# Attention, softplus FFN and routed experts on one core: wider mask and weight-conversion operations, setup on another engine, and a new table of due dates

## The chip, the cores and the metric

The program runs on one core of a Trainium2 chip. A core has TensorE (PE, matrix products), VectorE (DVE), ScalarE (ACT), GpSimd (POOL) and SyncE (SP, here the issuer of most transfers), each with an instruction stream of its own that it works through in order. The metric is the device time of the whole program in microseconds (us); lower is better.

## The reference, cut to what matters

```python
# attention: r, k, v are (4, 8, 768, 48), w and u (8, 48)
for t in range(S):
    cur = np.einsum('bhd,bhe->bhde', u[None] * kt, vt)
    y[:, :, t] = np.einsum('bhd,bhde->bhe', rt, state + cur)
    state = w[None, :, :, None] * state + np.einsum('bhd,bhe->bhde', kt, vt)
x = y, heads side by side: (3072, 384)
# FFN, w_in (384, 2048), w_out (2048, 384), both float64
h = x @ w_in
x = (np.maximum(h, 0.0) + np.log1p(np.exp(-np.abs(h)))) @ w_out
# experts: 8 of them, each takes at most 384 tokens, highest logits first
logits = x @ w_gate
(token, expert) pairs in falling order of logit; a token goes to the first expert with room
out[mask_e] = np.maximum(x[mask_e] @ w1[e], 0.0) @ w2[e]      # (384, 1024), (1024, 384)
```

## The kernel before

**Attention** is done in chunks of 64 time steps: 24 steps n, each for two sequences b and 8 heads (4 pairs `pr` of two, q = 0, 1). In a step PE transposes the scaled k and r (`ks`, `rs`) into `kT` and `ar`, `prods` makes 32 products of 64x64 (L516), DVE multiplies them by a triangular mask (`masked`, L524), and further products with `X` (L594) and the state follow. Three steps fill one block of 384 tokens.

**The FFN** takes 8 blocks of 384 tokens; for each of 16 slices f of the hidden size it makes 9 matmuls of 128x384 (L728; three in block 0, in fp32), softplus on ACT (L734 to L736) and DVE (L741, result `gf`), and a split of `gf` into two halves of 16 bits (L348 or L350, and `rest`, L748). The second product (L835 for block 0, L838 to L840) adds over the slices. `w_in` and `w_out` come as pairs of 32-bit words of a float64. `from_double` fetches one slice of 384 columns into one of four buffers `RAW` and makes float32 of it with three DVE operations on bits (L640, L642, L644): 32 slices, 96 operations. `halve_win` and `halve_wout` split the result into two fp16 halves.

**The experts** follow: `select(p)` finds the tokens of expert p by a search over thresholds (PE L1086, L1103, DVE L1073 to L1110), GpSimd gathers their rows (L1255), SP turns them by a transposing transfer (L1330), `up` makes 8 x 9 matmuls (L1342), `relu` (ACT L1346) and `rest` (DVE L1349) split the result, `down` makes 3 x 24 matmuls (L1360 to L1362), GpSimd scatters (L1370). The weights of an expert come in 8 pieces y (four of `w1`, four of `w2`) of 384 KB: `fetch` (SP, L1280) into one of four buffers `mraw` (`RB = 4`), which is free again when the piece four earlier has been converted; `hi` makes the upper half on ACT (L1289), `lo` the lower one on DVE (L1296). For the last two experts seven of the eight pieces are converted in another way (`ON_POOL`): ACT L1286 and L1287, then GpSimd L1294.

**What sets the order.** Nothing runs at once: each step is recorded as an item with an engine (or two that could take it, with a price each), a planned duration, what it depends on, and a due date. `lay_out` (L148) then simulates the engines with these durations and writes each engine's stream in the order that comes out; of the items that could start, the one with the earliest due date goes. Where two engines could take an item, `BIAS` and `YIELD` weigh one against the other. Transfers have a size, by which a single modelled DMA clock advances; an item without a size has a fixed delay `lat`:

```python
            if it.size:
                dma = max(start + 1275.0, dma) + it.size
                it.lat = dma + 1000.0 - it.done
```

`keep_warm` (L135) then puts filler matmuls (L143: zeros, into a bank that nobody reads) wherever the plan has PE idle. On the chip nothing of the plan is left but the order: an engine goes on when what it waits for is there. The plan's numbers stand in tables: `T0`, `LEN0`, `LEN`, `LAST` are the planned times of the FFN blocks, `RAWL`, `BITL`, `WOUTL`, `HALFL`, `HALFL2` how long before its use a weight is fetched, converted and split; `STEP` is the time per expert, `FETCHL`, `HIL`, `LOL`, `W1L`, `W2L` how long before its use a piece of expert weight is fetched and converted, `XLEAD` and `GLEAD` the leads of transposes and gathers.

At the start DVE makes the identities and the mask from an iota of GpSimd (`idents`, L418 to L421), then the table of powers of the decay w (`powers`, L427 to L436), of which PE transposes copies (L453, L459).

Of the kernel before, what the change touches and what calls it, by code (L numbers as in the profile page):

```python
# [21 lines left out]
def tile_kernel(ctx, tc, r, k, v, w, u, w_in, w_out, w_gate, w1, w2, out):  # L22
# [7 lines left out]
    C = 64  # L30
# [220 lines left out]
    T0 = 16250.0  # L251
    LEN0 = 43500.0
    LEN = 25600.0
    NLATE = 12
    EARLY = 0.62
    LATE = [divmod(NB * SPB - NLATE + i, SPB) for i in range(NLATE)]
    LAST = 26100.0
# [71 lines left out]
    RAW = [piece(flat, 4 * i, 4, I32).rearrange("p (m t) -> p m t", t=2) for i in range(4)]  # L329
    WT = [piece(flat, 22 + 2 * i, 2, FT) for i in range(3)]  # L330
# [66 lines left out]
    pw = AR[1].rearrange("p a b c d -> p (a b c d)")[:, :2 * HP * C].rearrange("p (i a c) -> p i a c", i=2, a=HP)  # L397
# [19 lines left out]
    def idents():  # L417
        DVE.tensor_scalar(identf, jp, 0.0, None, op0=OP.is_equal)  # L418
        DVE.tensor_copy(identh, identf)
        DVE.tensor_scalar(mask[0:64], jp[0:64, 0:64], 0.0, None, op0=OP.is_gt)  # L420
        DVE.tensor_scalar(mask[64:128], jp[64:128, 64:128], 0.0, None, op0=OP.is_gt)  # L421

    op("dve", 600.0, idents, r=["jp"], w=["ident"], due=-1e9)


    def powers():
        DVE.tensor_copy(sq[:, 0], wt)  # L427
        for i in range(6):
            DVE.tensor_mul(sq[:, i + 1], sq[:, i], sq[:, i])
        DVE.reciprocal(pw[:, 0, :, 0], sq[:, 5])  # L430
        DVE.tensor_copy(pw[:, 1, :, C - 1], pw[:, 0, :, 0])
        for i in range(6):
            m = 1 << i
            f = sq[:, i, :, None].to_broadcast([128, HP, m])
            DVE.tensor_mul(pw[:, 0, :, m:2 * m], pw[:, 0, :, 0:m], f)
            DVE.tensor_mul(pw[:, 1, :, C - 2 * m:C - m], pw[:, 1, :, C - m:C], f)  # L436
# [12 lines left out]
    op("dve", 3200.0, powers, r=["wt"], w=["pw", ("ar", 1, 0)], due=-1e8)  # L449

    def power_table(i):
        bank = Bank("att")
        op("dve", 335.0, lambda: DVE.tensor_copy(PW2[0], pw[:, i, :, None, :].to_broadcast([128, HP, 2, C])),  # L453
           r=["pw", ("ar", 1, 0)], w=["pw2", ("kT", 1)], due=-1e7)
# [14 lines left out]
    def attention(n):  # L469
# [41 lines left out]
        def prods():  # L511
            pa = [b.view(HP, 64) for b in b3]
# [13 lines left out]

        op("pe", 625.0, prods, r=[("kT", i), ("ar", i, 0), ("ar", i, 1)], w=[("am", i, 0), ("am", i, 1)], due=due + 3, bank=b3, small=True)
        for q in range(2):
            op("dve", 890.0, lambda q=q: masked(q), r=["ident"], w=[("am", i, q)], due=due + 3, bank=b3[q])
# [104 lines left out]
    def from_double(src, t, key, due):  # L634
        c = WN[0]
        WN[0] += 1
        raw = RAW[c % 4]
        op("sp", 450.0, lambda: src(raw), w=[("raw", c % 4)], due=due - RAWL, size=1900.0)
        hi, lo = [raw[..., i] if len(t.shape) == 2 else raw[..., i].rearrange("p (k f) -> p k f", k=KC) for i in (1, 0)]
        op("dve", 269.0, lambda: DVE.tensor_scalar(t, hi, 0x07FFFFFF, 3, op0=OP.bitwise_and, op1=OP.logical_shift_left),  # L640
           r=[("raw", c % 4)], w=[key], due=due - BITL)
        op("dve", 469.0, lambda: DVE.scalar_tensor_tensor(t, hi, -0x40000000, t, op0=OP.bitwise_and, op1=OP.bitwise_or),  # L642
           r=[("raw", c % 4)], w=[key], due=due - BITL)
        op("dve", 469.0, lambda: DVE.scalar_tensor_tensor(t, lo, 29, t, op0=OP.logical_shift_right, op1=OP.bitwise_or),  # L644
           r=[("raw", c % 4)], w=[key], due=due - BITL)

    def prep_win(j):
        from_double(lambda raw: SP.dma_start(
            raw.rearrange("p (k f) t -> p k (f t)", k=KC),
            w_in.rearrange("(k p) f -> p k f", p=128)[:, :, 256 * j:256 * (j + 1)]),  # L650
            WF32[j].bitcast(I32), ("wi", j + 1), due_ffn1(0, j))
# [10 lines left out]
    def prep_wout(f):  # L662
        due = due_ffn2(0, 0, f) - WOUTL
        t = WU32[f]
        from_double(lambda raw: SP.dma_start(
            raw.rearrange("p m t -> p (m t)"), w_out.rearrange("(c p) m -> c p m", p=128)[f]),
            t[:, :DM].bitcast(I32), ("wo", f + 1), due)
# [205 lines left out]
    for f in range(FC):  # L873
        prep_win(f)
# [114 lines left out]
    STEP = 25200.0  # L989
    SPAN = 22300.0  # L990

    ON_POOL = [()] * 6 + [(0, 1, 2, 3, 4, 5, 7)] * 2
    XLEAD = 10900.0
    GLEAD = 17400.0
    FETCHL = 20500.0
    W1L = -5700.0
    W2L = 9500.0
    HIL = 6100.0
    LOL = -11500.0
    DOWNL = 13200.0  # L1000
    INVL = -9500.0
# [247 lines left out]
    def gather(p, need):  # L1249
# [7 lines left out]
        for j in range(3):  # L1257
            old = xts[3 * p + j - 6] if p >= 2 else None
            GI[p].append(item("pool", 1050, lambda j=j: one(j), [SEL[p][3], old, more_room] + need, begin(p) - GLEAD, 2250))
            GI[p][-1].remote = True  # L1260

    def weights(p):
# [37 lines left out]
        for y in range(2 * WQ):  # L1300
# [3 lines left out]
            f = item("sp", 450, lambda y=y: fetch(y), [ld, old], want - FETCHL, size=1092)  # L1304
# [17 lines left out]
    def experts(p):  # L1322
# [90 lines left out]
        for j in range(3):  # L1413
# [11 lines left out]
            ots.append(item("pool", 1100, lambda j=j: scatter(j), [t], begin(p) + DOWNL + 3900 * (j + 1), 2300))  # L1425
# [43 lines left out]
```

## Time and profile before

| | |
|---|---|
| median of three runs | 768.3 us (767.6, 768.3, 773.15) |
| the profiled execution, as timed | 769.4 us |
| its span in the trace | 767.6 us |
| PE busy | 748.2 us, 97% |
| DVE busy | 593.8 us, 77% |
| ACT busy | 436.0 us, 57% |
| GpSimd busy | 80.1 us, 10% |
| granted TensorE clock, mean | 0.997 of full speed |

A line of the profile names an instruction by its line in the program (L524), its engine, its operation, what it writes and reads, and the partitions and elements of it. Busy time of PE counts fillers too, and the ends of matmuls are modelled, so that the busy share of PE says less than the distances between the starts of its instructions.

### The profile page before, as it was taken

Reading aid. Unit: us, or ns where it says so; the run is one execution under the profiler, and the core shown is the slowest. Engines: PE = TensorE matmul, PEld = TensorE weight load, DVE = VectorE, ACT = ScalarE, POOL = GpSimd, SP = SyncE. Lnnn points to the kernel's source line nnn. Section 1 sums busy time; section 2 is a strip of 40 time slices with the busy share of each in tenths; the row PEclk is TensorE's granted clock in tenths of the full one; section 3 lists DMA queues with packets and bytes.
Section 4 is the critical chain, followed back from the end, with each engine's and each line's share of the span. In section 5 each row is a group of like instructions: output and inputs, shape, how many; then the busy total and the mean of one; then the engine's idle time right before and its main releaser. Section 6 shows DMA issues by size and latency. Waiting matters only on the chain.

```text
span 767.6 us, 18561 instructions
## 1 busy us (share of the span) xinstructions
PE 748.2 (97%) x7322; PEld 493.1 (64%) x7322; DVE 593.8 (77%) x1643; ACT 436.0 (57%) x883; POOL 80.1 (10%) x110
## 2 busy tenths in 40 slices
PE   8999999999999999999999999999999999898996
PEld 8866676666666666667676666666766666555553
DVE  7999999997776776778987768787788889766220
ACT  4475777777666766768999902210343544326741
POOL 1000000000000000000000000000422131216731
PEclk9999999999999999999999999999999999999999
DMA  6895852442332333342200004242478383827810
GB/s 125 205 203 143 210 151 53 84 82 58 66 77 50 61 69 64 64 64 50 43 13 12 2 21 125 83 144 60 93 190 200 131 231 116 189 85 204 207 52 31
DMA packets 164982, 78.88 MB, mean 103 GB/s; under 512 B 130592, under 2 KB 160544, under 8 KB 164896
## 3 DMA queue, kind: packets, MB, share of 16 engines
q1 hardware_dynamic: 161824, 68.26, 38.7%
q0 software_dynamic: 3072, 9.44, 3.8%
q8 instruction: 57, 0.93, 0.5%
q14 instruction: 29, 0.24, 0.1%
HBM read 60.37 MB, written 9.63 MB: 91 GB/s over the span
## 4 chain that ended last, share of the span: by engine, by line
PE 62%; issue 13%; DVE 10%; ACT 6%; POOL 4%; DMA 3%; POOLq 0%; SPq 0%; DVEq 0%; ACTq 0%
PE bank L728 19%; PE bank L838 6%; PE bank L839 6%; PE bank L840 6%; PE bank L835 4%; PE bank L1342 3%; PE bank L594 3%; POOL out L1370 2%; PE bank L1086 1%; PE bank L516 1%; PE bank L1362 1%; PE bank L1360 1%; PE bank L143 1%; PE bank L1361 1%; PE bank L545 1%
## 5 line engine op out<-in xcount | busy, mean ns | idle before, releaser
L728 PEld LDWEIGHTS <-wi 128*128 128x128 f16 x1008 | 97.1, 98 | 66.6 <-issue 2.9
L728 PE MATMUL bank<-xt,wi 128*128 128x384 f16 x672 | 127.7, 327 | 0.1
L741 DVE SCALAR_TENSOR_TENSOR gf<-bank,ta 128x384 f32<-128x384 f32 x112 | 61.9, 555 | 31.6 <-ACT ta L736 30.7
L838 PE MATMUL bank<-wo,g 128*128 128x384 f16 (+1 forms) x240 | 78.6, 327 | 0.0
L840 PE MATMUL bank<-wo,g 128*128 128x384 f16 (+1 forms) x240 | 78.6, 327 | 0.0
L839 PE MATMUL bank<-wo,g 128*128 128x384 f16 (+1 forms) x240 | 78.6, 327 | 0.0
L734 ACT ACTIVATE ta<-bank 128x384 f32<-128x384 f32 x128 | 61.4, 482 | 29.5 <-PE bank L728 14.3
L728 PE MATMUL bank<-xs,wi 128*128 128x384 f16 x336 | 73.0, 326 | 0.0
L1342 PE MATMUL bank<-g,w1h 128*128 128x384 f16 x384 | 72.9, 326 | 0.0
L735 ACT ACTIVATE ta<-ta 128x384 f32<-128x384 f32 x128 | 66.8, 522 | 2.6
L736 ACT ACTIVATE ta<-ta 128x384 f32<-128x384 f32 x128 | 66.7, 521 | 2.5
L1362 PE MATMUL bank<-w2h,g 128*128 128x384 f16 x192 | 63.3, 330 | 2.7 <-DVE g L1349 2.6
L1360 PE MATMUL bank<-w2h,g 128*128 128x384 f16 x192 | 63.4, 330 | 1.1 <-ACT g L1346 1.1
L1361 PE MATMUL bank<-w2l,g 128*128 128x384 f16 x192 | 63.3, 330 | 0.0
L348 ACT ACTIVATE x2o<-bank 128x384 f16<-128x384 f32 x24 | 11.7, 488 | 80.0 <-PE bank L840 71.8
L748 DVE SCALAR_TENSOR_TENSOR g<-gf,g 128x384 f16<-128x384 f32 x80 | 44.2, 553 | 15.2 <-ACT g L348 14.7
L1346 ACT ACTIVATE g<-bank 128x384 f16<-128x384 f32 x64 | 30.7, 488 | 40.5 <-PE bank L1342 29.3
L1349 DVE SCALAR_TENSOR_TENSOR g<-bank,g 128x384 f16<-128x384 f32 x64 | 34.4, 548 | 21.5 <-ACT g L1346 21.3
L348 ACT ACTIVATE g<-gf 128x384 f16<-128x384 f32 x75 | 39.0, 520 | 20.1 <-DVE gf L741 19.8
L1342 PEld LDWEIGHTS <-w1h 128*128 128x128 f16 x384 | 35.8, 98 | 22.3
L524 DVE TENSOR_TENSOR ar<-bank,mask 64x256 f32<-64x256 f32 x96 | 40.5, 421 | 2.2
L1255 POOL DMA_INDIRECT third<-x2d,idx x24 | 25.6, 1066 | 157.3 <-DVE aj L1174 131.7
(234 smaller groups left out, 1535.7 us busy)
## 6 DMA issues: line engine op xcount, KB each, us to landing
mraw<-moe_w SPq DMA_DIRECT2D x64, 384.0 KB, 3.8
third<-moe_w_in SPq DMA_DIRECT2D x16, 384.0 KB, 4.8
third<-moe_w_out SPq DMA_DIRECT2D x16, 384.0 KB, 3.9
kn<-k SPq DMA_DIRECT2D x48, 96.0 KB, 2.9
rn<-r SPq DMA_DIRECT2D x48, 96.0 KB, 3.1
vn<-v SPq DMA_DIRECT2D x48, 96.0 KB, 3.1
x2d<-x2o SPq DMA_DIRECT2D x48, 96.0 KB, 2.2
X<-v SPq DMA_DIRECT2D x36, 96.0 KB, 3.3
```

The lines of the kernel that those rows point to most:

```text
L728: PE.matmul(ph, WF[:, f, a, kk, :], x[:, kk, :], start=(i == 0), stop=(i == 3 * KC - 1))
L734: op("act", 371.0, lambda: ACT.activation(ta, bank.view(BT), AF.Abs), w=[("ta", c)], due=due, bank=bank)
L735: op("act", 413.0, lambda: ACT.activation(ta, ta, AF.Exp, scale=-1.0), w=[("ta", c)], due=due)
L736: op("act", 413.0, lambda: ACT.activation(ta, ta, AF.Ln, bias=1.0), w=[("ta", c)], due=due)
L741: op("dve", 470.0, lambda: DVE.scalar_tensor_tensor(gf, bank.view(BT), 0.0, ta, op0=OP.max, op1=OP.add), r=[("ta", c)], w=[("gf", c)], due ...
L838: PE.matmul(p, gh[:, f, ts], WU[:, f, 0, :no], start=(f == 0), stop=False)
L839: PE.matmul(p, gh[:, f, ts], WU[:, f, 1, :no], start=False, stop=False)
L840: PE.matmul(p, gl[:, f, ts], WU[:, f, 0, :no], start=False, stop=(f == FC - 1))
L1342: PE.matmul(ph, a[:, kk, fs], XH[p][:, x0 + kk, :], start=(i == 0), stop=(i == 3 * KC - 1))
L1360: PE.matmul(po, h1h[:, f, js], w2h[:, fz, :], start=(f == 0), stop=False)
L1361: PE.matmul(po, h1h[:, f, js], w2l[:, fz, :], start=False, stop=False)
L1362: PE.matmul(po, h1l[:, f, js], w2h[:, fz, :], start=False, stop=(f == FB - 1))
```

## The change

Five things are done together.

1. In the first nine steps (`WHOLE = 9`) `masked` takes one DVE operation of 64x512 for each q in place of two of 64x256. For that, `prods` writes the products of both b of one q to the same 64 columns of the array (o = 1 - q), side by side in the bank, where it wrote those of b to columns of their own.
2. `from_double` takes two slices at once (768 columns, buffers `RAW2` over the old ones) for all but the first two slices of `w_in` and for all of `w_out`: 17 conversions of three operations in place of 32. The transfers of a pair of `w_in` remain two; a pair of `w_out` is one of 768 KB.
3. The identities and the mask are made on GpSimd. The table of powers is half as wide: 15 operations in place of 21 ahead of its first copy, the reversed half is read backwards, and the planner may give the copies to ACT.
4. In the planner's prices a fetch of expert weights takes 1700 in place of 1092 of the DMA clock, and gathers and scatters, which had a fixed delay of 2250 and 2300, advance it by 900; conversions on ACT and GpSimd for the last experts cost some 4% more.
5. The due dates, `BIAS` (0.43 to 1.348), `YIELD0` (400 to 248) and `SLACK` are new numbers.

```diff
-    LEN0 = 43500.0
-    LEN = 25600.0
+    LEN0 = 52137.908
+    LEN = 27173.331
...
-    STEP = 25200.0
+    STEP = 21647.984
...
-    HIL = 6100.0
-    LOL = -11500.0
+    HIL = 11584.279
+    LOL = 8711.69
...
+    RAW2 = [piece(flat, 8 * i, 8, I32).rearrange("p (m t) -> p m t", t=2) for i in range(2)]
...
+    def masks():
+        POOL.tensor_scalar(mask[0:64], jp[0:64, 0:64], 0.0, None, op0=OP.is_gt)
+        POOL.tensor_scalar(mask[64:128], jp[64:128, 64:128], 0.0, None, op0=OP.is_gt)
+        POOL.tensor_copy(identh, identf)
...
     def powers():
+        t = pw[:, :, C // 2:]
+        DVE.memset(t[:, :, 0], 1.0)
         DVE.tensor_copy(sq[:, 0], wt)
-        for i in range(6):
+        DVE.tensor_copy(t[:, :, 1], wt)
+        for i in range(5):
+            m = 2 << i
             DVE.tensor_mul(sq[:, i + 1], sq[:, i], sq[:, i])
...
+            if i < 4:
+                DVE.tensor_mul(t[:, :, m:2 * m], t[:, :, 0:m], sq[:, i + 1, :, None].to_broadcast([128, HP, m]))
+        DVE.reciprocal(rec, sq[:, 5])
+        DVE.tensor_mul(pw[:, :, :C // 2], t, rec[:, :, None].to_broadcast([128, HP, C // 2]))
+        DVE.tensor_mul(sq[:, 6], sq[:, 5], sq[:, 5])
...
-                        PE.matmul(pa[q][b * 64:(b + 1) * 64, pr, :],
+                        o = (1 - q if n < WHOLE else b) * 64
+                        to = b3[q].view(HP, 2, 64)[:, pr, b] if n < WHOLE else pa[q][:, pr]
+                        PE.matmul(to[o:o + 64],
...
         def masked(q):
             o = 1 - q
+            if n < WHOLE:
+                rows = slice(o * 64, (o + 1) * 64)
+                DVE.tensor_mul(ar[rows, :, :, q, :], b3[q].view(HP, 2, 64)[rows],
+                               mask[rows, None, None, :].to_broadcast([64, HP, 2, 64]))
+                return
...
+        raw = RAW[c % 4] if m == 1 else RAW2[c // 2 % 2]
+        raws = [("raw", (c + i) % 4) for i in range(m)]
+        op("sp", 450.0 * m, lambda: src(raw), w=raws, due=due - RAWL, size=1900.0 * m)
...
-            f = item("sp", 450, lambda y=y: fetch(y), [ld, old], want - FETCHL, size=1092)
+            f = item("sp", 450, lambda y=y: fetch(y), [ld, old], want - FETCHL, size=1700)
...
-            GI[p].append(item("pool", 1050, lambda j=j: one(j), [SEL[p][3], old, more_room] + need, begin(p) - GLEAD, 2250))
+            GI[p].append(item("pool", 1270, lambda j=j: one(j), [SEL[p][3], old, more_room] + need, begin(p) - GLEAD, size=900.0))
```

Three engines show what becomes of the order. A row is an instruction's line, its operation, and what it writes and reads with the shape; the lines of the changed kernel are higher by 8 to 22.

**DVE, around the masks of the third step.** Before, each mask is two operations (x2), and the weights (`wi`) are converted in threes of 128x384, here with two slices interleaved:

```order
L642 SCALAR_TENSOR_TENSOR wi_133<-third_130,wi_133 128x384
L640 TENSOR_SCALAR wi_133<-third_130 128x384
L644 SCALAR_TENSOR_TENSOR wi_133<-third_130,wi_133 128x384
L524 TENSOR_TENSOR ar0_111<-bank4_84,mask_143 64x4x64 x2
L524 TENSOR_TENSOR ar0_111<-bank3_83,mask_143 64x4x64 x2
L642 SCALAR_TENSOR_TENSOR wi_133<-third_130,wi_133 128x384
```

Now:

```order
L659 SCALAR_TENSOR_TENSOR wi_133<-third_130,wi_133 128x384
L532 TENSOR_TENSOR ar0_111<-bank0_80,mask_143 64x8x64
L532 TENSOR_TENSOR ar0_111<-bank1_81,mask_143 64x8x64
L359 COPY X2_99<-vn0_95 64x192
L595 TENSOR_TENSOR sv0_107<-vn0_95,bank3_83 128x384
L359 COPY X2_99<-vn0_95 64x192
L655 TENSOR_SCALAR wi_133<-third_130 128x768
```

A mask is one operation of twice the width, and the conversion that follows is one of a pair.

**ACT, in the sixth expert.** `w1h` and `w2h` are conversions (`hi`), `g10` the results of `relu`, `g11` those of `down`. Before, from the last two slices of `w1h` to the outputs:

```order
L1289 ACTIVATE w1h_8837<-mraw_8782 128x768
L1346 ACTIVATE g10_128<-bank6_86 128x384
L1346 ACTIVATE g10_128<-bank2_82 128x384
L1289 ACTIVATE w1h_8887<-mraw_8802 128x768
L1346 ACTIVATE g10_128<-bank0_80 128x384
L1289 ACTIVATE w2h_8908<-mraw_8848 128x768
L1346 ACTIVATE g10_128<-bank3_83 128x384
L1346 ACTIVATE g10_128<-bank1_81 128x384
L1346 ACTIVATE g10_128<-bank6_86 128x384
L348 ACTIVATE g11_129<-bank5_85 128x384
```

Now:

```order
L1311 ACTIVATE w2h_8641<-mraw_8541 128x768
L1368 ACTIVATE g10_128<-bank2_82 128x384
L1368 ACTIVATE g10_128<-bank4_84 128x384
L1368 ACTIVATE g10_128<-bank1_81 128x384
L1311 ACTIVATE w1h_8697<-mraw_8571 128x768
L1368 ACTIVATE g10_128<-bank0_80 128x384
L1311 ACTIVATE w1h_8735<-mraw_8623 128x768
L351 ACTIVATE g11_129<-bank5_85 128x384
L351 ACTIVATE g11_129<-bank6_86 128x384
L1311 ACTIVATE w2h_8827<-mraw_8744 128x768
```

Of the conversions among the results of `relu`, the one of `w2h` that had three of them behind it stands ahead of them all now; two of `w1h` have moved in between the last ones, with one result of `relu` behind the first.

**SP, at the same expert.** A fetch writes `mraw`, a DMA_TRANSPOSE is a turn of gathered rows, an ISA row belongs to the fetch behind it. Before:

```order
L1280 DMA mraw_8802<-moe2_w1 128x3x256
L1330 DMA_TRANSPOSE g11_129<-third_130 128x6x128 x2
L1280 ISA
L1280 DMA mraw_8848<-moe2_w2 128x2x384
L1330 DMA_TRANSPOSE g11_129<-third_130 128x6x128
L1280 ISA
L1280 DMA mraw_8874<-moe2_w2 128x2x384
```

Now:

```order
L1302 DMA mraw_8541<-moe2_w2 128x2x384
L1352 DMA_TRANSPOSE g11_129<-third_130 128x6x128
L1302 ISA
L1302 DMA mraw_8571<-moe2_w1 128x3x256
L1352 DMA_TRANSPOSE g11_129<-third_130 128x6x128
L1302 ISA
L1302 DMA mraw_8623<-moe2_w1 128x3x256
L1352 DMA_TRANSPOSE g11_129<-third_130 128x6x128
L1302 ISA
L1302 DMA mraw_8744<-moe2_w2 128x2x384
```

The fetch that stood behind two transposes (`mraw_8848`) has two fetches of `w1` in its place, each behind a transpose, and the fetches of `w2` for the expert at work stand ahead of all three.

## Rows read from the trace of the kernel before

**Rows 1.** Busy time by stretch; per engine PE, PEld, DVE, ACT, POOL; then PEclk, DMA share, GB/s.

```profile
8.00:100.00 92.00, 88.83 (x1157) 64.91 (x1155) 87.05 (x208) 57.83 (x126) 0.00 (x0) 1.00 0.79 189
100.00:173.00 73.00, 72.48 (x802) 48.90 (x800) 70.73 (x160) 55.59 (x125) 0.82 (x2) 1.00 0.41 84
173.00:435.00 262.00, 261.56 (x2955) 172.77 (x2954) 201.65 (x487) 204.67 (x438) 1.90 (x9) 1.00 0.27 51
...
660.00:680.00 20.00, 16.81 (x114) 10.01 (x113) 10.51 (x37) 4.39 (x9) 1.07 (x2) 0.91 0.39 111
761.00:767.60 6.60, 0.00 (x0) 0.00 (x0) 0.00 (x0) 0.49 (x1) 0.96 (x1) 0.90 0.08 30
```

**Rows 2.** Waits of DVE, 8 to 100 us, the longest sum: us, times, longest.

```profile
DVE ar L356 <- ACT ar L354: 1.3, 2, 0.7
```

**Rows 3.** Fillers: group (busy, mean ns); two stretches; a run in the last chain.

```profile
L143 PE MATMUL bank<-still 128*128 128x128 bf16 x402 | 34.1, 229 | 1.0 <-DVE wt L400 1.0
...
8.00:100.00 92.00, 13.33 (x177) 10.77 (x174) 1.00 0.79 189
100.00:173.00 73.00, 7.99 (x105) 6.66 (x105) 1.00 0.41 84
...
104.80 2.46 PE bank L143 x44
```

**Rows 4.** Groups by shape, a DVE copy: busy us, mean ns | idle before.

```profile
L356 DVE COPY ar<-bank 64x512 f32<-64x512 f32 x11 | 7.6, 689 | 3.0 <-ACT ar L354 2.9
```

**Rows 5.** DVE in order of time: start, us; near 14, 105, 176 (the 17th gf) and 558 us.

```profile
13.98 1.77 DVE L524 TENSOR_TENSOR ar<-bank,mask 64x256 f32<-64x256 f32 x4
...
105.33 0.56 DVE L343 TENSOR_TENSOR sv<-vn,sd 128x384 f32<-128x384 f32 x1
105.80 0.36 DVE L640 TENSOR_SCALAR wo<-third 128x384 int32<-128x384 int32 x1
106.07 0.56 DVE L741 SCALAR_TENSOR_TENSOR gf<-bank,ta 128x384 f32<-128x384 f32 x1
...
175.77 0.55 DVE L741 SCALAR_TENSOR_TENSOR gf<-bank,ta 128x384 f32<-128x384 f32 x1
...
557.94 0.94 DVE L1296 SCALAR_TENSOR_TENSOR w1l<-mraw,w1h 128x768 f16<-128x768 f32 x1
558.80 0.15 DVE L1107 TENSOR_REDUCE dm<-bank 128x1 f32<-128x8 f32 x1
```

**Rows 6.** The same at the start: the last mask and the last power.

```profile
2.74 0.71 DVE L421 TENSOR_SCALAR mask<-jp 64x64 f32<-64x64 int32 x1
...
6.36 0.29 DVE L436 TENSOR_TENSOR ar<-ar,sq 128x128 f32<-128x128 f32 x1
```

**Rows 7.** The chain that ended last: products of 128x64 and of 64x64.

```profile
120.54 1.07 PE bank L594 x32
...
357.78 0.77 PE bank L516 x32
```

**Rows 8.** Waits of PE from 640 us on: us, times, longest.

```profile
PE bank L1086 <- DVE cmp L1073: 3.2, 1, 3.2
PE bank L1362 <- DVE g L1349: 2.6, 1, 2.6
PE bank L1360 <- ACT g L1346: 1.1, 1, 1.1
```

**Rows 9.** Instructions in order of time, 654 to 700 us; SPq is SP's queue.

```profile
654.89 7.44 SPq L1330 DMA_TRANSPOSE g<-third  x2
...
666.17 0.84 ACT L1289 ACTIVATE w2h<-mraw 128x768 f16<-128x768 f32 x1 [3.83 <-DMA mraw<-moe_w]
666.92 1.23 ACT L1346 ACTIVATE g<-bank 128x384 f16<-128x384 f32 x3
...
696.59 5.39 DVE L1165 TENSOR_SCALAR si<-sl 128x24 int32<-128x24 f32 x1
697.08 3.25 POOL L1294 TENSOR_TENSOR w1l<-mraw,w1h 128x768 f16<-128x768 f32 x2
```

More of the change, by code (lines that the diff above doesn't have):

```diff
@@ L415, in tile_kernel @@
     op("pool", 700.0, pads, w=["pads"], due=-1e9)
[L417 to L423, printed above, removed]
+    def masks():
+        POOL.tensor_scalar(mask[0:64], jp[0:64, 0:64], 0.0, None, op0=OP.is_gt)
+        POOL.tensor_scalar(mask[64:128], jp[64:128, 64:128], 0.0, None, op0=OP.is_gt)
+        POOL.tensor_copy(identh, identf)
+    op("pool", 800.0, lambda: POOL.tensor_scalar(identf, jp, 0.0, None, op0=OP.is_equal), r=["jp"], w=["ident"], due=-1e9)
+    op("pool", 1500.0, masks, r=["jp", "ident"], w=["mask"], due=-1e9)
     def powers():
+        t = pw[:, :, C // 2:]
+        DVE.memset(t[:, :, 0], 1.0)
         DVE.tensor_copy(sq[:, 0], wt)
-        for i in range(6):
+        DVE.tensor_copy(t[:, :, 1], wt)
+        for i in range(5):
+            m = 2 << i
             DVE.tensor_mul(sq[:, i + 1], sq[:, i], sq[:, i])
[L430 to L436, printed above, removed]
+            if i < 4:
[3 more added lines that the diff above has]
+        DVE.tensor_mul(sq[:, 6], sq[:, 5], sq[:, 5])
     uw = const.tile([128, HP, 2], FT, name="uw")
@@ L511, in prods @@
         def prods():
-            pa = [b.view(HP, 64) for b in b3]
+            pa = None if n < WHOLE else [b.view(HP, 64) for b in b3]
             for pr in range(HP):
@@ L632, in tile_kernel @@
     WN = [0]
[L634 to L651, printed above, removed]
+    def from_double(src, view, keys, due, shape):
+        m = len(keys)
+        c = WN[0] if m == 1 else WN[0] + WN[0] % 2
+        WN[0] = c + m
+        raw = RAW[c % 4] if m == 1 else RAW2[c // 2 % 2]
+        raws = [("raw", (c + i) % 4) for i in range(m)]
+        op("sp", 450.0 * m, lambda: src(raw), w=raws, due=due - RAWL, size=1900.0 * m)
+        hi, lo = [shape(raw[..., i]) for i in (1, 0)]
+        op("dve", 69.0 + 200.0 * m, lambda: DVE.tensor_scalar(view, hi, 0x07FFFFFF, 3, op0=OP.bitwise_and, op1=OP.logical_shift_left),
+           r=raws, w=keys, due=due - BITL)
+        op("dve", 69.0 + 400.0 * m, lambda: DVE.scalar_tensor_tensor(view, hi, -0x40000000, view, op0=OP.bitwise_and, op1=OP.bitwise_or),
+           r=raws, w=keys, due=due - BITL)
+        op("dve", 69.0 + 400.0 * m, lambda: DVE.scalar_tensor_tensor(view, lo, 29, view, op0=OP.logical_shift_right, op1=OP.bitwise_or),
+           r=raws, w=keys, due=due - BITL)
@@ L653, in halve_win, with prep_win, load @@
+    def prep_win(j, m):
+        def load(raw):
+            for i in range(m):
+                SP.dma_start(raw[:, i * DM:(i + 1) * DM].rearrange("p (k f) t -> p k (f t)", k=KC),
+                             w_in.rearrange("(k p) f -> p k f", p=128)[:, :, 256 * (j + i):256 * (j + i + 1)])
+        from_double(load, WF[:, j + 1:j + 1 + m].rearrange("p j a k f -> p (j a k f)").bitcast(I32),
+                    [("wi", j + 1 + i) for i in range(m)], due_ffn1(0, j), lambda h: h)
     def halve_win(j):
@@ L872, in tile_kernel @@
         attention(n)
-    for f in range(FC):
-        prep_win(f)
+    for f in range(SINGLE):
+        prep_win(f, 1)
+    for f in range(SINGLE, FC, 2):
+        prep_win(f, 2)
     for f in range(FC):
@@ L1424, in experts @@
             pos.append(t)
-            ots.append(item("pool", 1100, lambda j=j: scatter(j), [t], begin(p) + DOWNL + 3900 * (j + 1), 2300))
+            ots.append(item("pool", 1200, lambda j=j: scatter(j), [t], begin(p) + DOWNL + 3900 * (j + 1), size=900.0))
             ots[-1].remote = True
```

73 lines of the change are left out of this document (39 added, 34 removed).

## The prediction

> **What bounds the kernel now.** First the page's engine line, in the table above: PE is busy 97% of the span, DVE 77%. That is an average over stages, so the second view is busy time by stretch [rows 1]. From 8 to 100 us DVE works 87.05 of 92 us and from 100 to 173 us 70.73 of 73; from 173 to 435 us only 201.65 of 262, while PE has no pause at all. So the third view, the waits of DVE: up to 100 us the longest sum is 1.3 us, for ACT [rows 2]. DVE is the bound of the front, and it waits for hardly anything there. PE is "busy" in the front too, but with fillers: of 402 in the program, 282 stand between 8 and 173 us, and a run of 44 takes 2.46 us, so 0.056 us each [rows 3]. These 282 are 15.8 us in which PE does nothing of use. From 173 us on PE is the bound, and what it lost before is never regained: every microsecond that DVE gains in the front moves the end, up to the point at which PE has no idle time left.
>
> In the experts PE is the bound again, except for three waits of 3.2, 2.6 and 1.1 us [rows 8]. The first goes back to SP: two transposes hold its stream for 7.44 us from 654.89, so the fetch behind them goes at 662.3 at the earliest, ACT starts its conversion at 666.17 after idling 3.83 us, and three results of `relu` stand behind that conversion on ACT [rows 9]. The stretch from 660 to 680 us has a mean granted clock of 0.91 [rows 1], so part of it at the lower of the two levels (1.2 and 2.4 GHz); PE had paused there. The second: a DVE operation on 24 columns took 5.39 us from 696.59, while GpSimd did subtractions from 697.08 on [rows 9]; the next `rest` stood behind it. The last 6.6 us [rows 1] are the last output and its scatter, which no edit shortens.
>
> **Edits in the front, on DVE.** What counts is the distance between starts, since operations overlap at their ends: one of 384 columns is shown with 0.56 us, but the next starts 0.47 us later, and the bit operation L640 takes 0.27 of its 0.36 [rows 5].
>
> Masks: the four of a step take 1.77 us, without overlap [rows 5]. A 64x512 copy out of a bank takes 0.689 us [rows 4]; two of these are 1.38 to 1.45 us, so a step saves 0.32 to 0.39, nine steps 3 us. The ends: nothing, if the wide one costs twice 0.44, and 5.3 us, if it overlaps its neighbour by as much as the 384-wide ones do.
>
> Pairs: two slices cost 2 x (0.27 + 0.47 + 0.47) = 2.42 us now. An operation of 768 columns with two inputs starts its successor 0.86 us later [rows 5]; for the one-input one I have no row and take 0.47, the 0.27 plus half of what the other gains with the width. That is 2.19, so a pair saves 0.23 and 15 pairs 3.4 us.
>
> Powers: 21 operations from the end of the last mask at 3.45 to 6.65 us [rows 6], 0.15 each; six fewer save 0.9, less the wider last one, say 0.8, on the chain on which everything starts. The masks of rows 6 and the identities leave DVE, which then waits for the decay to land instead of for itself: 0.
>
> Together DVE has 7.2 us less to do. What of that reaches PE depends on the order, so I counted each order's DVE instructions up to a common mark, the results `gf` of block 1 (the first block with splits), each at the distance its shape has in the trace ([rows 5] shows such shapes; before there are 1643 DVE instructions, after 1594), and PE's useful matmuls up to the same marks. Up to the 17th `gf`: 165.9 us of DVE work before, 157.6 after, with the same PE work (136.9 us at its matmuls' usual distances). Up to the 21st: 172.8 and 172.2, but with PE 3.0 us further on. In the trace the 17th came at 175.77 us [rows 5], so DVE idled about 10 us in all. With the same idle time after, PE is ahead by 8.3 us at the first mark and by 7 to 8 at the second, where PE has become the bound. **I take 8 us.** The fillers say the same by another way: the order after has 224 of them, 178 fewer, and 178 x 0.056 = 10.0 us. Ends: 3 us, if half the saving goes into new waits for the loads, which now bring two slices before a conversion may start, and 10.
>
> Products: the 32 of a step take 0.77 us; the nearest row with only two blocks of the array at work is L594, 32 in 1.07 [rows 7]. Nine steps then cost PE 0.3 x 9 = 2.7 us, and at most 6.9 if they double. In these steps PE has the fillers' 15.8 us to spare, so I cost it at 0; where a product is itself waited for by DVE, part of the 2.7 comes through. The Trainium skill, TensorEngine Tiling (Array Packing), section Tiling Modes, counts four independent tiles in the 64x64 mode, which speaks against bringing them down to two; by it the 32 products would double. No row shows that form; by the rule the sum changes only if the cover of the fillers goes.
>
> **Edits in the experts.** The low halves are due 20 us earlier (LOL), so a fetch buffer comes free sooner, and each fetch has a higher price in the plan. In the order the `w2` fetches of the expert at work now stand ahead of the three transposes, and the conversion that had three `relu` results behind it precedes them. Its wait of 3.2 us goes, and with it the low clock, 0.09 x 20 = 1.8 us. What is late next are the two `w1h` conversions whose fetches stand behind a transpose each; only one `relu` stands behind them, so I leave 1 us for that: 4 us regained. Of the other two waits (3.7 us) the GpSimd subtractions for experts 7 and 8 keep runs of two and three, so I take back 1 only. **Together 5 us**; ends 0 and 8. GpSimd's and SP's other moves (gathers, scatters) are behind waits for work that PE does anyway: 0.
>
> **The sum.** The profiled execution took 769.4 us (span 767.6), 1.1 above the median. 769.4 - 8 - 5 = 756.4, and on the footing of the median 755.3: **755 us**.
>
> **Rivals.**
>
> *The front's gain turns into waits.* DVE has less to do, but what it needs comes no sooner: loads of two slices before one conversion, or DVE waiting for ACT. For it: DMA is busy 0.79 of 8 to 100 us [rows 1]. Against: DVE waits for a load hardly ever now. Front 2, experts 5: 761.
>
> *The experts' waits stay*, at other places: transposes still stand ahead of fetches on SP, and the runs on GpSimd are left. Front 8, experts 0: 760.
>
> *It does nothing:* fillers go, and PE waits instead, for the same DVE; experts as now: 767. Against it stands the count at the 17th mark.
>
> *GpSimd slows DVE at the start.* A short DVE operation lasts 5.39 us beside GpSimd's subtractions [rows 9]. The setup now runs on GpSimd while DVE makes the powers; if DVE stood still for as long as the four operations took there (at most 4 x 0.71 = 2.8 [rows 6]), the chain of the start would be 2.0 longer instead of 0.8 shorter: 758. Against: the transfer of the decay is waited for anyway. The Trainium skill, GPSIMD Engine Reference, section 8. Key points, says that GpSimd shares its SBUF interfaces with VectorE and contends with instructions that have two SBUF inputs, as the powers do; the trace agrees that there is such a thing, though the operation there has one input.
>
> *Slower: a piece of weights late in every expert.* Fetches stand between the transposes on SP, and each waits for a buffer that a conversion must free; in turn the next transpose waits, and PE cannot begin the next expert. One such event costs what the first wait did, 3.2 + 1.8 = 5 us. Two of them leave part of the gain of 13; from 13 / 5, three, the kernel is slower than before, with four it takes 755 + 4 x 5 = 775, and with one in each of the seven later experts 790. For it: the transposes' SP time of 7.44 us. Against: in the trace one expert of eight had it.
>
> **Chances.** Forecast 0.50 (750 to 758), experts' waits stay 0.17, front's gain lost 0.12, slow start 0.08, nothing 0.06, slower 0.07. A measurement of this kernel can tell about 1% from no change, that is 760.6 and 776. Faster by more: forecast, slow start and half of the cases at 760 to 761: 0.72. Slower by more: 0.07. Within: 0.21. The range goes from 746 (front 10, experts 8, and 4 more if DVE idles 6 us instead of 10) to 767, where nothing is gained, and leaves out the slower case.
>
> **What would show it.** Right: fillers 224 and PE's starts from 180 us on earlier by about 8 us against the same `gf`; DVE still over 94% busy from 8 to 150 us; masks at about 0.7 us, bit operations of 768 at 0.95; in the experts no PE wait over 2 us but one beside a run of L1316 on GpSimd, and a clock of 1.00 around the sixth. Wrong: PE idle for DVE or for `third` loads in the front where the fillers were; a wide mask above 0.88 us; a PE wait of 3 us in several experts with SP's transposes ahead of it. The forecast rests most on DVE's idle time staying at 10 us in the front: if it doubles, the front's gain is gone.

## The result, and the profile after

The changed kernel takes 759.4 us (median of four runs, 759.17 to 759.91), the kernel before beside it 770.3 (767.6 to 773.15): ratio 0.986, interval 0.982 to 0.990. The forecast was 755, 1.7% below the 768.3 of the first three runs; measured is 1.4%. Of the 13 us forecast the front gave what it should and the experts hardly any.

The first view is busy time by stretch, of the changed kernel; the columns are those of [rows 1].

```profile
8.00:100.00 92.00, 89.25 (x1233) 67.32 (x1231) 86.46 (x171) 64.29 (x142) 0.00 (x0) 1.00 0.81 183
100.00:173.00 73.00, 72.48 (x640) 46.49 (x638) 71.66 (x156) 50.99 (x114) 0.82 (x2) 1.00 0.45 100
173.00:435.00 262.00, 261.93 (x2973) 173.73 (x2967) 208.05 (x506) 196.44 (x422) 2.09 (x9) 1.00 0.25 48
...
660.00:680.00 20.00, 20.00 (x143) 12.31 (x142) 17.00 (x58) 9.90 (x16) 6.62 (x7) 1.00 0.41 129
680.00:700.00 20.00, 14.47 (x81) 8.24 (x80) 11.40 (x21) 6.58 (x11) 9.95 (x9) 0.83 0.58 148
...
752.00:758.10 6.10, 0.00 (x0) 0.00 (x0) 0.00 (x0) 0.10 (x1) 0.96 (x1) 0.64 0.09 32
```

DVE is as full as before up to 173 us: it is still the bound there, and what it does in that time is worth more. From 660 to 680 us PE now runs without a pause at full clock; from 680 to 700 it works 14.47 of 20 us at a granted clock of 0.83. The pause of before in 660 to 680 us is gone, and another stands from 684 us on.

The fillers, as in [rows 3]: the group, and the two stretches.

```profile
L143 PE MATMUL bank<-still 128*128 128x128 bf16 x224 | 22.5, 239 | 1.0 <-DVE ar L432 1.0
...
8.00:100.00 92.00, 10.27 (x117) 7.65 (x114) 1.00 0.81 183
100.00:173.00 73.00, 1.31 (x6) 0.59 (x6) 1.00 0.45 100
```

123 of them stand between 8 and 173 us, 282 before: 159 x 0.056 = 8.9 us that PE does not spend on zeros.

DVE in order of time, at the start and at the masks of the first step:

```profile
3.44 0.43 DVE L433 COPY sq<-wt 128x4 f32<-128x4 f32 x1 [2.48 <-DMA wt<-w]
...
5.71 0.15 DVE L442 TENSOR_TENSOR sq<-sq 128x4 f32<-128x4 f32 x1
5.82 0.43 DVE L359 COPY kT<-ar 128x512 f32<-128x512 f32 x1
7.72 0.26 DVE L359 COPY X<-vn 64x192 f32<-64x192 f32 x1 [1.47 <-DMA vn<-v]
8.01 0.43 DVE L359 COPY kT<-ar 128x512 f32<-128x512 f32 x1
...
14.14 1.41 DVE L532 TENSOR_TENSOR ar<-bank,mask 64x512 f32<-64x512 f32 x2
15.47 0.54 DVE L595 TENSOR_TENSOR sv<-vn,bank 128x384 f32<-128x384 f32 x1
```

The powers end at 5.86 us in place of 6.65 [rows 6]. The second copy of the table stands behind a copy that waits 1.47 us for a load, and starts at 8.01; before it started at 7.86, behind a wait for PE:

```profile
7.86 0.43 DVE L453 COPY kT<-ar 128x512 f32<-128x512 f32 x1 [0.75 <-PE bank L459]
```

The two masks of a step take 1.33 us to the next start, where four took 1.78 to 1.81 in most steps of the trace before (1.72 in the one of [rows 5], whose 1.77 is from the first start to the last end). The groups of the new shapes:

```profile
L532 DVE TENSOR_TENSOR ar<-bank,mask 64x512 f32<-64x512 f32 x18 | 12.4, 688 | 0.7 <-PE bank L524 0.2
L657 DVE SCALAR_TENSOR_TENSOR wi<-third,wi 128x768 int32<-128x768 int32 x7 | 6.6, 949 | 0.1
L655 DVE TENSOR_SCALAR wi<-third 128x768 int32<-128x768 int32 x7 | 3.8, 548 | 0.0
```

The 32 products of a step on PE, in order of time, a step of before and one of now:

```profile
17.55 0.70 PE L516 MATMUL bank<-ar,kT 64*64 64x64 f32 x32
```

```profile
12.40 1.15 PE L524 MATMUL bank<-ar,kT 64*64 64x64 f32 x32
```

What PE waits for from 530 us on, a line as in [rows 8]:

```profile
PE bank L1214 <- DVE rv L1199: 5.5, 1, 5.5
```

And DVE, GpSimd and PE around it in order of time:

```profile
683.45 5.51 DVE L1196 TENSOR_TENSOR aj<-jj,sqd 128x144 bf16<-128x144 f32 x1
...
683.97 1.65 POOL L1316 TENSOR_TENSOR w1l<-mraw,w1h 128x768 f16<-128x768 f32 x1
...
685.57 3.22 POOL L1316 TENSOR_TENSOR w2l<-mraw,w2h 128x768 f16<-128x768 f32 x2
...
689.00 0.54 DVE L1199 TENSOR_TENSOR rv<-aj,val 128x144 bf16<-128x144 bf16 x2
...
689.59 0.85 PE L1214 MATMUL bank<-rv,cmi 128*128 128x24 bf16 x12 [5.53 <-DVE rv L1199]
...
690.56 0.53 PE L1383 MATMUL bank<-w2l,g 128*128 128x384 f16 x1
```

A DVE operation that takes 0.29 to 0.30 us in the other experts lasts 5.51 us and ends 0.17 us after a run of three subtractions on GpSimd. It belongs to the selection of the last expert. PE's next instruction (L1214) needs `rv`, which DVE makes from the result of the held operation, so PE stands for 5.5 us. Behind the pause the matmuls of 384 columns start 0.32 us apart up to 695.6 us, and 0.162 apart after it: for 5 us the clock is at the lower of its two levels, which costs 2.5 us. It is the mechanism of [rows 9], with another operation of DVE held and PE close behind it.

A correction to the words ahead of this section: by PE's marks the expert that they call the sixth, with the first wait, is the fifth of eight; the collision stands in the sixth, before and after, while GpSimd converts the seventh's weights.

### The profile page after: what moved, and what is told of

Read it like the earlier page. It is cut to its first block, busy times and chain, and to the rows that moved or that the text cites. A ratio compares the mean times of both kernels' runs of the same rounds, so it can differ in the third digit from the quotient of the medians.

```text
span 758.1 us, 18115 instructions
## 1 busy us (share of the span) xinstructions
PE 741.5 (98%) x7144; PEld 489.2 (65%) x7144; DVE 595.1 (79%) x1594; ACT 424.2 (56%) x859; POOL 85.2 (11%) x114
## 4 chain that ended last, share of the span: by engine, by line
PE 71%; DVE 15%; issue 5%; DMA 3%; POOL 2%; ACT 2%; SPq 1%; POOLq 0%; DVEq 0%; ACTq 0%
PE bank L748 19%; PE bank L1364 9%; PE bank L858 6%; PE bank L860 6%; PE bank L859 6%; PE bank L1382 3%; PE bank L1383 3%; PE bank L1384 3%; PE bank L607 2%; PE bank L1108 2%; PE bank L855 2%; PE bank L524 1%; DMA third<-moe_w_in 1%; PE bank L558 1%; SPq L373 1%
## 5 line engine op out<-in xcount | busy, mean ns | idle before, releaser
L748 PEld LDWEIGHTS <-wi 128*128 128x128 f16 x1008 | 97.9, 98 | 66.0 <-issue 2.3
L748 PE MATMUL bank<-xt,wi 128*128 128x384 f16 x672 | 127.6, 326 | 0.1
L754 ACT ACTIVATE ta<-bank 128x384 f32<-128x384 f32 x128 | 61.4, 483 | 36.3 <-PE bank L748 25.1
L748 PE MATMUL bank<-xs,wi 128*128 128x384 f16 x336 | 72.9, 326 | 0.0
L1364 PE MATMUL bank<-g,w1h 128*128 128x384 f16 x384 | 72.9, 326 | 0.0
L1364 PEld LDWEIGHTS <-w1h 128*128 128x128 f16 x384 | 35.7, 98 | 22.1
L351 ACT ACTIVATE x2o<-bank 128x384 f16<-128x384 f32 x24 | 11.6, 489 | 67.5 <-PE bank L860 41.5
L1277 POOL DMA_INDIRECT third<-x2d,idx x24 | 27.6, 1151 | 156.7 <-PE bank L1125 132.3
L351 ACT ACTIVATE g<-gf 128x384 f16<-128x384 f32 x66 | 34.3, 520 | 16.2 <-DVE gf L761 16.0
L1364 PE MATMUL bank<-g,w1l 128*128 128x384 f16 x192 | 41.7, 326 | 0.0
```

What stands on the lines that cost most here:

```text
L748: PE.matmul(ph, WF[:, f, a, kk, :], x[:, kk, :], start=(i == 0), stop=(i == 3 * KC - 1))
L754: op("act", 371.0, lambda: ACT.activation(ta, bank.view(BT), AF.Abs), w=[("ta", c)], due=due, bank=bank)
L1364: PE.matmul(ph, a[:, kk, fs], XH[p][:, x0 + kk, :], start=(i == 0), stop=(i == 3 * KC - 1))
```

## The experiments

The runs are compared by marks of their traces as well as by their times: the start of the 17th `gf`, the start of the last matmul of the first FFN product (L728, after L748), PE's end, and the wait of ACT for weights (`mraw`) from 540 us on. A ratio stands against the kernel before in the same set of runs; between sets that kernel itself went from 769.0 to 776.6 (the set of e1 to e4), so that ratios of different sets agree to about 1% only. Its marks are those of its one trace, an execution of 769.4 us. The same kernel's marks in two sets (the changed one, e5) agree to 0.2 us.

| kernel | median us | ratio, interval | fillers | 17th gf | last FFN-1 matmul | PE's end | between the two | longest PE wait in the experts | ACT waits for mraw |
|---|---|---|---|---|---|---|---|---|---|
| before | 770.3 | 1 | 402 | 175.8 | 436.3 | 761.0 | 324.7 | 3.2 | 12.9 |
| changed | 759.4 | 0.986 (0.982 to 0.990) | 224 | 168.3 | 428.6 | 751.6 | 323.0 | 5.5 | 0 |
| e1 code, old table | 768.1 | 0.988 (0.984 to 0.991) | 246 | 169.1 | 430.5 | 759.8 | 329.3 | 2.8 | 16.8 |
| e2 table, old code | 762.4 | 0.981 (0.978 to 0.985) | 436 | 177.7 | 437.6 | 753.7 | 316.1 | 0.8 | 0.7 |
| e3 two masks | 762.3 | 0.981 (0.978 to 0.985) | 277 | 169.5 | 430.0 | 753.5 | 323.5 | 5.5 | 0.5 |
| e4 single slices | 770.1 | 0.991 (0.987 to 0.994) | 334 | 174.5 | 436.5 | 761.8 | 325.3 | 5.5 | 0.2 |
| e5 changed again | 759.9 | 0.986 (0.980 to 0.991) | 224 | 168.1 | 428.5 | 751.5 | 323.0 | 5.5 | 0 |
| e6 seventh off GpSimd | 752.1 | 0.977 (0.971 to 0.982) | 224 | 167.8 | 427.9 | 742.9 | 315.0 | 0.3 | 2.2 |
| e7 no GpSimd | 752.4 | 0.977 (0.972 to 0.982) | 224 | 168.0 | 428.5 | 743.8 | 315.3 | 0.3 | 2.3 |
| e8 every second piece | 758.1 | 0.984 (0.979 to 0.989) | 224 | 168.2 | 428.5 | 748.9 | 320.4 | 3.6 | 1.4 |
| e9 old expert table | 761.3 | 0.990 (0.986 to 0.994) | 231 | 168.0 | 428.3 | 751.2 | 322.9 | 3.6 | 12.3 |
| e10 setup as before | 761.0 | 0.988 (0.986 to 0.991) | 241 | 169.9 | 430.0 | 752.8 | 322.8 | 5.5 | 0 |
| e11 before, seventh off GpSimd | 768.6 | 0.998 (0.996 to 1.000) | 402 | 175.1 | 436.8 | 761.5 | 324.7 | 2.1 | 21.4 |
| e12 pairs cut | 761.6 | 0.990 (0.986 to 0.994) | 224 | 170.7 | 430.9 | 753.2 | 322.3 | 5.5 | 0 |

**Code or table (e1, e2).** e1 is the changed code with every number and price of before, of which the diff shows three; e2 is the reverse in the kernel before:

```diff
-    BIAS = 1.348
+    BIAS = 0.43
...
-    LEN0 = 52137.908
+    LEN0 = 43500.0
...
-    LOL = 8711.69
+    LOL = -11500.0
```

e1, expected:

> The changed code (wide masks, pairs, setup on GpSimd, short powers) with every number of the table and every price as before. Theory A, less DVE work makes the front faster: counted up to the 17th gf DVE has 157.3 us of work in this order against 165.9 before, up to the 21st 165.4 against 172.8, so the last matmul of the first FFN product comes 7 to 8 us earlier than before (428 to 429 us); with the experts as before the time is 760 to 763. Theory B, the new due dates make the gain and the edits alone give little: 766 to 770. The rival that wide products (1.15 us in place of 0.70 a step) cost PE what DVE gains says 765 and more.

e2, expected:

> The code of before with all the new numbers and prices. Theory A: DVE has 169.7 us of work ahead of the 17th gf (165.9 before) and 181.0 ahead of the 21st (172.8), and 436 fillers stand in the order (402 before), so the front loses 2 to 6 us and the experts are as with the change: 769 to 774. Theory B: 760 to 763, as the whole change.

In the front theory A has the direction right for both and the size too large: the last FFN matmul comes 5.8 us earlier with the code alone (430.5; 7 to 8 were expected) and 1.3 later with the table alone (437.6; 2 to 6). What is left of the time of the 17th `gf` when the counted DVE work is taken off is nearly the same in every order: 157.3 + 11.8 in e1, 169.7 + 8.0 in e2, 157.6 + 10.7 in the changed kernel, 165.9 + 9.9 before. DVE's pauses up to that mark, added up in the traces, are 12.7, 8.2, 11.6 and 9.5 us, so the rest is idle time to within 1 us. Both expected times failed all the same: e1 took 768.1 us, not 760 to 763, and e2 762.4, not 769 to 774. For e1 that depends on the measure: in its own set, where the kernel before took 776.6, its ratio of 0.988 is what 760 to 763 would have been against 770. By the traces the miss lies in the experts. From the last FFN matmul to PE's end e1 takes 329.3 us where 324.7 (as before) was expected, and e2 only 316.1 where 323.0 (as with the change) was. So in the front the code gives the gain, and the table's worth lies in the experts.

The chief wait of e1 is that of [rows 9] again; the rows are ACT's, in order of time:

```profile
664.73 0.84 ACT L1311 ACTIVATE w2h<-mraw 128x768 f16<-128x768 f32 x1 [4.00 <-DMA mraw<-moe_w]
665.48 0.85 ACT L1368 ACTIVATE g<-bank 128x384 f16<-128x384 f32 x2
```

e2 has a run of three on GpSimd too, and DVE at work beside it unharmed; both in order of time:

```profile
694.68 1.67 POOL L1294 TENSOR_TENSOR w1l<-mraw,w1h 128x768 f16<-128x768 f32 x1
...
695.67 0.32 DVE L1201 TENSOR_REDUCE idx<-tok 64x3 int32<-64x6 f32 x2
...
696.02 1.02 DVE L1349 SCALAR_TENSOR_TENSOR g<-bank,g 128x384 f16<-128x384 f32 x2
...
696.29 3.24 POOL L1294 TENSOR_TENSOR w2l<-mraw,w2h 128x768 f16<-128x768 f32 x2
```

Two `rest` operations, with one operand in a bank, take 1.02 us as ever, and two short reductions 0.32 as they do elsewhere. No operation of the kind that was held before stands beside this run.

**Masks (e3)**, `WHOLE = 9` to 0, which brings back the masks and the products of before. Expected:

> The changed kernel with the masks and products of before (WHOLE = 0), all else as changed. Theory A: DVE has 0.7 us more ahead of the 17th gf and 1.0 more ahead of the 21st; the products get 0.45 us faster in nine steps, 4 us, but PE has spare time there: 760 to 762, 0.5 to 2 us more than the changed kernel. Rival, the wide products are the dearer part: 755 to 758, faster than the changed kernel.

The 17th `gf` comes 1.2 us later than in the changed kernel and the last FFN matmul 1.4: theory A, though the time, 762.3, is a little more than the 762 expected at most. The products are at 0.69 us a step again, and PE gains nothing from it.

**Pairs (e4, e12).** e4 converts each slice by itself (`SINGLE = FC`, and the single load of `w_out`). Expected:

> The changed kernel with every weight slice converted by itself, as before. Theory A: DVE has 163.6 us ahead of the 17th gf against 157.6, 175.6 against 172.2 ahead of the 21st: 3 to 6 us more than the changed kernel, 762 to 766. Rival, loads of two slices make conversions late and the width brings nothing: 757 to 760.

The 17th `gf` is 6.2 us later, as counted (6.0), and the last FFN matmul 7.9, all that the front had gained. The time, 770.1, is beyond the 762 to 766 of the theory, and the 7.9 us are twice what the width can give. So e12 keeps the changed kernel's order on every engine, and its loads, and cuts only the operations (`each` takes the two halves in turn; one of the three is shown):

```diff
-        op("dve", 69.0 + 400.0 * m, lambda: DVE.scalar_tensor_tensor(view, hi, -0x40000000, view, op0=OP.bitwise_and, op1=OP.bitwise_or),
+        op("dve", 69.0 + 400.0 * m, lambda: each(lambda v, h: DVE.scalar_tensor_tensor(v, h, -0x40000000, v, op0=OP.bitwise_and, op1=OP.bitwise_or), view, hi),
```

Expected:

> The changed kernel in its own order on every engine, with the loads of two slices, but each of the three bit operations of a pair done as two of 384 columns. If the gain of the pairs is the width alone, as counted in the prediction (0.23 us a pair, 15 pairs, 3.4 us), the 17th gf comes 3 to 3.5 us later than in the changed kernel (168.2) and the last FFN matmul at 431 to 432 us (428.5), 762 to 764 in all. If it is the whole 8 us that converting slice by slice cost (last FFN matmul at 436.5), it comes at 435 or later; if the width brings nothing and the order all, at 429 or earlier.

The 17th `gf` comes at 170.7, 2.4 us later, and so does the last FFN matmul (2.4 against 428.5). The width is worth 2.4 us, a little less than the 3 to 3.5 expected. The other 5.5 us of e4 are its order and its loads of single slices, which no run takes apart: with 32 conversions in place of 17 the same due dates lead the planner to another order, in which, among other moves, 15 splits of `w_out` stand ahead of the 17th `gf` in place of 12, and 9 copies of `X` in place of 6.

**GpSimd in the experts (e5 to e8).** e6 and e7 shorten one list:

```diff
-    ON_POOL = [()] * 6 + [(0, 1, 2, 3, 4, 5, 7)] * 2
+    ON_POOL = [()] * 7 + [(0, 1, 2, 3, 4, 5, 7)]      # e6
+    ON_POOL = [()] * 8                                # e7
+    ON_POOL = [()] * 6 + [(0, 2, 4, 6), (0, 1, 2, 3, 4, 5, 7)]   # e8
```

e5, expected:

> The changed kernel itself, as the measure for the runs beside it: 758 to 762, with a wait of PE of about 5.5 us for a DVE operation that ends with a run of three subtractions on GpSimd.

e6, expected:

> The changed kernel with the seventh expert's weights converted on ACT and DVE as those of the first six; only the last expert's use GpSimd. Theory P, a DVE operation with its operands in SBUF is held until GpSimd's run of subtractions ends and PE waits for it: the wait of 5.5 us goes, and with it the low clock behind it, 5.5 plus 2 to 3 us: 751 to 754. Rival Q, the wait is the selection or the weights coming late, and GpSimd only happens to run then: another wait of 3 us or more takes its place, 757 to 761.

e7, expected:

> The changed kernel with no weight conversion on GpSimd at all. Theory P: as the run without it in the seventh expert, 751 to 754, since no selection runs beside the last expert and DVE has time there. Rival Q: 757 to 761. If DVE becomes the bound in the last two experts: 755 and more.

e8, expected:

> The changed kernel with only the pieces 0, 2, 4 and 6 of the seventh expert on GpSimd, so that no three of its subtractions follow each other. Theory P: a held DVE operation waits 1.7 us at most, PE's longest wait in the experts is under 2 us, 752 to 755. Rival Q: 757 to 761 with a wait above 3 us.

e6 removes the wait and 8.0 us between the last FFN matmul and PE's end: 5.5 of wait and 2.5 of low clock. Busy time by stretch of e6, and PE's longest wait from 520 us on:

```profile
680.00:700.00 20.00, 20.00 (x133) 12.35 (x132) 11.31 (x25) 8.37 (x14) 10.74 (x13) 1.00 1.06 209
```

```profile
PE bank L1407 <- DMA third<-x2d,idx: 0.3, 1, 0.3
```

At 752.1 us e6 is the fastest kernel here, 2.3% below the kernel before (1.8 to 2.9). e7 is its equal: no selection runs beside the last expert, and GpSimd's conversions there hold nobody up in e6. e8 missed theory P's number: 758.1 with a wait of 3.6 us is what rival Q said. But its pieces, which were meant to stand singly, still stood two in a row; DVE and GpSimd in order of time, and PE's longest wait:

```profile
683.35 3.87 DVE L1196 TENSOR_TENSOR aj<-jj,sqd 128x144 bf16<-128x144 f32 x1
...
683.81 1.65 POOL L1316 TENSOR_TENSOR w1l<-mraw,w1h 128x768 f16<-128x768 f32 x1
...
685.40 1.64 POOL L1316 TENSOR_TENSOR w2l<-mraw,w2h 128x768 f16<-128x768 f32 x1
```

```profile
PE bank L1214 <- DVE rv L1199: 3.6, 1, 3.6
```

So beside a run of three the operation takes 5.51 us, beside a run of two 3.87, and without a run 0.3: the wait follows the length of the run, as theory P has it. Q, that weights or the selection are late by themselves, would have left a wait in e6.

**The expert part of the table (e9)**, STEP to INVL and the prices as before, in the changed kernel. Expected:

> The changed kernel with the expert part of the table (STEP to INVL) and the prices of fetches, gathers and scatters as before. The order has again a fetch of w2 for the expert at work behind two transposes. If the due dates of the expert part removed the first wait, a wait of about 3 us for selection behind a late conversion comes back in the sixth expert or beside it; the last FFN matmul stays at 428 to 429 us, and from it to PE's end it takes 325 us or more, as before (324.7), in place of 323.0: 761 to 765. Rival, the first wait went because the front shifted the experts: no such wait, 752 to 760, by the collision with GpSimd alone.

The median of 761.3 falls into the range of the first theory, but not for its reason; the traced execution, the fastest of the four at 759.6, falls into the rival's, and takes 322.9 us from the last FFN matmul to PE's end, as the changed kernel does. ACT waits 12.3 us for weights again (0 in the changed kernel), though no one wait of 3 us for the selection comes back (0.7 is the most). The wait of 3.6 us is GpSimd's again: DVE's L1189 takes 5.36 us from 687.36 beside a run of three. The experts up to the end of the fifth take 2.8 us more (428.3 to 673.1, against 428.6 to 670.6). So neither theory stands as it was put: the old table brings late weights in each kernel that has it (12.3 to 21.4 us of ACT's waits, 2.3 or less without it), but how much of that reaches PE depends on where it falls.

**Setup (e10)**, identities, mask and long table on DVE as before. Expected:

> The changed kernel with identities and mask on DVE and the long table of powers, as before. Theory A: the first copy of the table comes 0.8 us later, but the copy behind it waited for a load anyway: 0 to 1 us more than the changed kernel at the last FFN matmul (428.5), so 428 to 430. Rival, GpSimd's setup slows DVE: 427 or earlier.

The last FFN matmul comes at 430.0, 1.5 us later, and the 17th `gf` 1.8. The edit is worth that, a little more than the 0 to 1 expected; GpSimd does not slow DVE on balance.

**The kernel before with the seventh expert off GpSimd (e11).** Expected:

> The kernel before with the seventh expert's weights converted on ACT and DVE. Theory P: its wait of 2.6 us behind a held DVE operation and the one of 1.1 us behind late conversions on ACT go, 3 to 6 us less than before (ratio 0.992 to 0.996), while the wait of 3.2 us in the sixth expert stays. Rival Q: no difference beyond 1 us, ratio 0.999 to 1.003.

The wait of 2.6 us is gone, the first wait is 2.1 us where 3.2 were expected to stay, and the sixth expert takes 25.8 us from the fifth's last matmul to its own (28.5 before). The ratio 0.998 lies in the range of neither theory: the seventh takes 28.0 for 25.1. ACT waits 3.23 us for a weight there, two waits of PE for `relu` follow, 2.0 us together where one of 1.1 stood before, and the granted clock from 720 to 740 us is 0.91 (1.00 before), which is 1.8 us more. ACT, then PE, each in order of time:

```profile
718.09 0.84 ACT L1286 ACTIVATE mraw<-mraw 128x768 f32<-128x768 f32 x1 [3.23 <-DMA mraw<-moe_w]
```

```profile
725.48 0.34 PE L1360 MATMUL bank<-w2h,g 128*128 128x384 f16 x1 [1.06 <-ACT g L1346]
```

With the old table late weights take away what GpSimd gives back. That they are late because of this edit is not shown.

## Why the prediction was right in the front and short in the experts

**Front: 8 us forecast, 7.7 measured** (436.3 to 428.6). The count of DVE work up to a common mark was the step that carried it: 8.3 forecast at the 17th `gf`, 7.5 measured, with DVE's idle time at 10.7 us for an assumed 10. The fillers said 10.0 by all of them; those of 8 to 173 us give 8.9.

Its terms: *masks* take 0.688 us each and start the next thing after 0.667, both means, so a step saves 1.79 (four times 0.449) - 1.33 = 0.46 us, nine 4.1, between the 3 taken and the upper end of 5.3; of that 1.4 reaches PE (e3, ordered anew). *Pairs*: 768 columns with two inputs are 0.868 us apart and the one-input form 0.469, the 0.86 and 0.47 that the estimate took; 3.4 us forecast, 2.4 by e12. *Powers*: 0.8 us shorter, as forecast, at the end of the table; the next copy lost it to a load ahead of it in DVE's stream, and yet e10 puts the whole setup at 1.5 us. *Products*: 1.15 us a step, in six of the nine, for 0.70; 0.45 x 9 = 4.1 us, inside the bounds of 2.7 and 6.9, and hidden, as costed (e3). The Trainium skill, TensorEngine Tiling (Array Packing), section Tiling Modes, counts four tiles in the 64x64 mode, from which the prediction worked out a doubling for two; the trace shows a factor of 1.6.

**Experts: 5 us forecast, 1.7 measured** (324.7 to 323.0). Two of its steps were right. The fifth expert, from its first matmul of `up` (L1342, now L1364) to the next expert's, takes 25.8 us in place of 30.3: 4.5 regained, 4 forecast. The third wait went as well. The step that failed is this one: "Of the other two waits (3.7 us) the GpSimd subtractions for experts 7 and 8 keep runs of two and three, so I take back 1 only." It saw that the runs stay, but priced the collision at no more than it had cost before. It grew: the sixth expert takes 33.6 us in place of 28.6. Before, a `rest` that PE needed later stood four operations behind the held one, and PE lost 2.6 us, with a clock of 1.00 from 700 to 720 us. Now only the two operations of L1199 stood between the held one and a PE instruction, and PE lost the whole hold, 5.5 us, and 2.5 by the clock after. What such a hold costs is between nothing and the run's length plus the clock, whatever it cost in the order before: the changed kernel has two shorter ones, 1.77 and 1.13 us beside single subtractions at 675 and 678 us, behind which PE does not wait at all. DVE in order of time:

```profile
674.41 0.29 DVE L1196 TENSOR_TENSOR aj<-jj,sqd 128x144 bf16<-128x144 f32 x1
...
674.74 1.99 DVE L1199 TENSOR_TENSOR rv<-aj,val 128x144 bf16<-128x144 bf16 x2
...
678.29 1.13 DVE L1156 TENSOR_TENSOR closed<-closed,esel 128x8 f32<-128x8 f32 x1
```

Of the signs that the prediction names for being right, those that the traces can show came: 224 fillers, starts of PE about 8 us earlier, DVE 95.5% busy from 8 to 150 us, masks of 0.688 us and bit operations of 0.949, a full clock from 660 to 680 us, and one PE wait over 2 us, beside a run of L1316. So the wait was foreseen as a sign, and its size was missing from the sum.

**Rivals.** "The experts' waits stay" (760, chance 0.17) came nearest: the 759.4 lies 1.4 us above the forecast's own band of 750 to 758. Of the two causes that this rival names the runs on GpSimd made the wait, and the transposes did not; and the experts gave 1.7 us, not 0. "GpSimd slows DVE at the start" did not decide anything: the first copies are stretched (0.43 us for 0.17), the chain is shorter all the same. The Trainium skill, GPSIMD Engine Reference, section 8. Key points, names contention of GpSimd with DVE instructions that have two SBUF inputs or run in a 2-port mode; the runs agree in the experts: operations with two inputs in SBUF (L1196, L1199) are held, and of those with one input some are (L1165, [rows 9]), while those with an operand in a bank (L1349 in e2) are not. The reductions in e2, with one input in SBUF, were not held either; what mode any of them ran in, no trace shows. The slower case, a late piece in every expert, did not occur: ACT never waits for weights.

Not settled is how much of the first wait's going is the table and how much the shift of the experts by 8 us: e9 has neither the wait nor the prompt weights.

## What to carry to other kernels

Where one engine is full and another behind it idles or spins, count the full engine's work ahead of a common mark in both orders, at the distances between starts from the trace; here, with the 10 us of idle time of the order before, that gave the 17th `gf` to within 2 us in five other orders (the changed kernel and e1 to e4), and found the one that lost. Price a collision of two engines by what it can cost, the whole length of the run that holds plus the clock that falls behind the pause, not by what it cost in the old order; better, take one of the two engines off the work, which here gave 8.0 us where the whole change had given 1.7 in the experts. Look at what stands behind it, though: the same edit in the kernel before (e11) gave 0.2%, since other waits filled the place. Judge edits and due dates apart: the same code with the old dates and the same dates with the old code were 5.8 us earlier and 1.3 later in the front, and in the experts the other way round.

## What the runs showed of the hardware that was not expected

A DVE operation that starts just ahead of a GpSimd subtraction can be held until the whole run of subtractions ends, through the seams between them: 5.36 to 5.52 us for runs of three (nine traces), 3.87 for a run of two. It is held although it starts 0.46 to 0.52 us ahead of GpSimd's shown start and needs only 0.3; GpSimd's shown starts are rough. It is not always held: in the changed kernel the same L1196 started 0.46 us ahead of a single subtraction and took its usual 0.29, and the second L1199 behind it took 1.77. What decides between the two is not shown.

DVE operations on 64x256 out of a bank stand 0.449 us apart at a duration of 0.422, so they do not overlap. Of the two masks of 64x512 in a step the first does not overlap either (0.725 apart at 0.694) and the second does (0.607 at 0.682); 0.667 and 0.688 are the means. So a pair of wide masks gains 0.12 us more by the second one, for a reason that no run shows.
